# Moving a 288-byte table behind the big tiles: the same program with most on-chip addresses 96 bytes lower

## The chip, the cores and the metric

The kernel runs on one core of a Trainium2 chip. The metric is the device time of one execution in microseconds; the median of several runs is compared. A core has a matmul engine (TensorE, PE in the profile, with its weight loads as PEld), VectorE (DVE), ScalarE (ACT), GpSimd (POOL) and SyncE (SP). Each has a queue of its own, in which instructions start in order, and they wait for each other by semaphores. On-chip memory has 128 partitions; a tile occupies the same range of bytes in each of them. Transfers are issued from SP's, ACT's and POOL's queues and run on the 16 DMA engines of the core.

## The reference

Attention with a window of 128 keys and four sink keys, and then a mixture of four experts, in which every token uses all four, weighted by its gates.

```python
# q, k, v: (4, 8, 768, 64); domain_probs: (3072, 4); w1: (4, 512, 1024); w2: (4, 1024, 512)
scores = q @ k.T / sqrt(64)                       # per batch and head
keep = (key < 4) | ((0 <= query - key) & (query - key < 128))
a = softmax(where(keep, scores, -1e9))
x = (a @ v) as (3072, 512)                        # heads side by side
p = domain_probs / (domain_probs.sum(-1, keepdims=True) + 1e-9)
for e in range(4):
    out += p[:, e:e+1] * (relu(x @ w1[e]) @ w2[e])
```

## The kernel before

**Order of the work.** The kernel text is a planner. While it is built it keeps an estimated clock for each engine (the dictionary t), and at each step emits the piece of work that is ready and has the best priority: a step of attention, a first product (x by w1), or a second product (the hidden rows by w2). So the order on each engine is fixed when the program is built, from constants alone. Nothing in it looks at an address.

**Stages.** The four batches are worked through in turn, each in three groups of 256 tokens. Rows of q and k are loaded by GpSimd into the tiles qkn (L267, 128 bytes of bf16 per head and token) and, from the second batch on, turned into qkT by DMA transposes that SP issues (L276). Rows of v go to the six tiles vx (L331), in which a head takes 66 elements, 132 bytes. Scores come from L719, their exponent from L747 into aT, the masks from L739, the products with v from L789 into od; ACT scales them into onat (L834), and a DMA transpose makes xT (L806). For most units (256 tokens by one expert) both products are computed in a form with seven partial products instead of eight: L1336 and L1224 are first products of this kind, L1511 the second ones into acc. The sums that it needs are formed by VectorE: L1384 and L1399 in the first product, L1451 and L1428 on the hidden rows in H.

**Turned units.** A unit of later batches is either computed with hidden features in partitions, and then its gates are a row tile (gates0, filled by L491), or turned: with tokens in partitions. Then the gate of a token is one number per partition, read from the table own_gates at L1357 (ACT) or L1361 (DVE), and the finished half unit is brought into H by a DMA transpose at L1317. Its source is one of a few half-unit tiles: row, rest, or lent space of gates. own_gates is loaded once, when attention reaches the second batch, at L1634, and normalised by four short VectorE instructions.

**Spaced row loads.** For the later batches GpSimd places a copy of two elements into the tile held before each row load (L212 and L1726). The copy reads something that another engine has just made, and so holds the load back until then.

**Tiles.** Pools are laid out in the order in which they are opened: consts, wpool, attn_sb, moe_sb, odd. Within a pool tiles follow each other in the order of their creation, each rounded up to 32 bytes. The pool consts holds vx0 to vx5 (1,056 bytes each), own_gates (288), the row gates, ident, masks and the sink keys. Then come the weights, the attention tiles and the mixture's tiles, nearly all of 256 bytes times a whole number, and behind them, in odd, what is small or uneven.

The lines at the centre, cut where dots stand, with their numbers:

```python
325     vx = [consts.tile([P, H, DP], BF16, name=f"vx{tb}") for tb in range(NQB)]
327     own_gates = consts.tile([P, OWNED, E], FP32, name="own_gates")
...
276     nc.sync.dma_start(out=qkT[b][:, :, :, tb * P:(tb + 1) * P]..., in_=nat[b, tb]..., transpose=True)
331     nc.gpsimd.dma_start(out=vx[tb][:, :, 0:D], in_=v[b, :, tb * P:(tb + 1) * P, :].rearrange("h p d -> p h d"))
...
1317    nc.sync.dma_start(out=H[:, k]..., in_=X[k]..., transpose=True)
1361    nc.vector.tensor_scalar(out=X[k][:, :, s], in0=src, scalar1=0.0, scalar2=gate, op0=ALU.max, op1=ALU.mult)
1384    nc.vector.tensor_add(tiles["V"], c5, tiles["X"])
1451    x[0](*x[1:])          # one of three sums: S0 = H21 + H22, S1 = S0 - H11, H21 = H11 - H21
```

The unit's tiles["V"] of L1384 is what the products P7 and P3 of the same unit are added to, so PE waits for it. L1451 runs when all of H has landed.

Of the kernel before, what the change touches and what calls it, by code (L numbers as in the profile page):

```python
# [11 lines left out]
FP32 = mybir.dt.float32  # L12
BF16 = mybir.dt.bfloat16
# [3 lines left out]
def kernel(  # L17
# [17 lines left out]
    E, Dm, F = moe_w1.shape  # L35
    Ntok, Dout = out.shape

    P = 128
# [7 lines left out]
    NHP = H // 2  # L46
# [52 lines left out]
    NEARLY = 2  # L99
# [39 lines left out]
    def dve(cols, *deps, rate=0.96, fixed=157):  # L139
        at = max([t["dve"], *deps])  # L140
        t["dve"] = at + fixed - 77 + cols / rate
        return at + fixed + 60 + cols / rate

    def pool(cols, *deps, fixed=190):
        at = max([t["pool"], *deps])
        t["pool"] = at + fixed + cols * 1.8
        return t["pool"] + 35
# [96 lines left out]
    consts = ctx.enter_context(tc.tile_pool(name="consts", bufs=1))  # L244
# [3 lines left out]
    odd = ctx.enter_context(tc.tile_pool(name="odd", bufs=1))  # L248
# [75 lines left out]

    vx = [consts.tile([P, H, DP], BF16, name=f"vx{tb}") for tb in range(NQB)]
    OWNED = 2 * NG * (B - OWN)
    own_gates = consts.tile([P, OWNED, E], FP32, name="own_gates")

    def load_v(b, ts):
        for tb in ts:  # L330
            nc.gpsimd.dma_start(  # L331
                out=vx[tb][:, :, 0:D],
                in_=v[b, :, tb * P:(tb + 1) * P, :].rearrange("h p d -> p h d"),
            )
            lands(("v", b, tb), H * P, D, values_at[b - 1, min(NG - 1, (tb + 1) // 2)] if b else 0.0)
# [159 lines left out]
        gate_at[pair, e] = sp(mix.finished[mix.gated[len(gate_sb) - 1 - NGATE]] if len(gate_sb) > NGATE else 0.0, takes=300) + GATE_LANDS  # L495


    held = odd.tile([P, 2], BF16, name="held")
    nc.vector.memset(identf, 1.0)
    lent = wpool.tile([P, 12 * P], BF16, name="lent", tag=f"wf_{E - 2}")  # L500
    zeros = lent[:, 0:4 * P]
# [4 lines left out]
    for h in range(H):  # L506
# [1 line left out]
        nc.sync.dma_start(  # L508
            out=vsf[r:r + NSINK, :, 0:D], in_=v[:, h, 0:NSINK, :].rearrange("b j d -> j b d"),
        )  # L510
    scale_t = odd.tile([P, 2 * NEARLY, E], FP32, name="scale_t")
    ident = consts.tile([P, P], BF16, name="ident")
    load_v(0, (0,))
    for sgn in (1, -1):
# [2 lines left out]
            base=0, pattern=[[sgn, P]], channel_multiplier=-sgn,  # L517
        )
        pool(0, fixed=320)
    sel2 = odd.tile([P, NHP, 2], FP32, name="sel2")  # L520
    load_v(0, (1,))
    t["sw"] += 500
    for tb in (2, 3):
# [52 lines left out]
    t["dve"] += 240.0  # L576

    vsd = {}
    half = odd.tile([P, 2], BF16, name="half")
    ksd = [consts.tile([P, NHP, 32], BF16, name=f"ksd{i}") for i in range(2)]  # L580

    nc.vector.memset(half, 0.0)
# [375 lines left out]


    def gates():  # L960
        rs = odd.tile([P, 2 * NEARLY], FP32, name="rs")
        nc.vector.reduce_sum(out=rs, in_=scale_t, axis=AX.X)
        nc.vector.tensor_scalar_add(out=rs, in0=rs, scalar1=1e-9)
        nc.vector.reciprocal(out=rs, in_=rs)
        nc.vector.tensor_mul(scale_t, scale_t, rs[:, :, None].to_broadcast([P, 2 * NEARLY, E]))
        dve(200)
# [8 lines left out]
    class Mixture:  # L975
# [608 lines left out]
        def emit_second(self):  # L1584
            ready = self.second_ready()
            g, s, e = self.second.pop(0)
            if g not in out_sb:
                out_sb[g] = mo.tile([P, 2, Dout], FP32, name="osbw", tag=f"wide{g}", bufs=1)
                if g == 0:
                    gates()  # L1590
# [232 lines left out]
```

## Time and profile before

| what | value |
|---|---|
| median of the runs | 353.84 us (353.64 to 354.11) |
| the profiled execution | 356.82 us, of which the span is 355.1 |
| granted TensorE clock | 1.00 |
| instructions | 8,924 |
| moved by DMA | 47.95 MB in 173,606 packets, 158,084 of them under 512 bytes |
| DMA queue of GpSimd (q0) | 79,104 packets, 56.9% of 16 engines' span |
| DMA queue of SP (q1) | 93,404 packets, 47.3% of 16 engines' span |

The page of a profile gives the busy time of each engine, the span in 40 slices with the busy share in tenths, the DMA queues, the chain of work that ended last, and the costliest groups of instructions, each by its line, engine, operation and tiles. The two shares of the DMA queues can add up to more than the busy time of the engines, since the packets of one queue take longer when the other's are served between them. The span runs from the first to the last instruction; the time of an execution is a little longer.

### The profile page before, as it was taken

To read this page: it belongs to the slowest core of one execution; us is meant where nothing else is said; L and a number is where in the kernel's file an instruction comes from. 1 tells how busy PE (TensorE), PEld (TensorE's weight loads), DVE (VectorE), ACT (ScalarE), POOL (GpSimd) and SP (SyncE) were. 2 spreads that over 40 slices of the span, in tenths; PEclk is the share of its full clock that TensorE was granted. 3 is DMA by queue.
4 is the path that set the end of the run, shared out by engine and by line. 5 is a ranking of instruction groups with operands and counts; after the bars stand their busy time and mean duration, and the time that the engine had idled before them with its cause. 6 is when DMAs were issued, how large, how long until landed. Compare 5 with 4: busy or idle time off the path is not lost. (4 is left out here: it accounts for less than half of the span.)

```text
span 355.1 us, 8924 instructions
## 1 busy us (share of the span) xinstructions
PE 344.3 (97%) x3439; PEld 256.0 (72%) x3470; DVE 276.0 (78%) x661; ACT 215.5 (61%) x491; POOL 80.6 (23%) x125
## 2 busy tenths in 40 slices
PE   7999999999999999999999979999999999999996
PEld 3685769756788978786997736855856666666785
DVE  5792999988998999798699479669859595685740
ACT  4865714447656576658545569489678666757511
POOL 8946114330452540800252110000000000000000
PEclk9999999999999999999999999999999999999999
DMA  9999999999997999994899957538527938455431
GB/s 173 173 189 194 220 207 172 170 152 162 172 110 77 170 181 170 145 121 41 95 190 111 167 105 144 95 83 141 104 73 145 162 70 160 79 97 141 85 95 61
DMA packets 173606, 47.95 MB, mean 135 GB/s; under 512 B 158084, under 2 KB 169572, under 8 KB 173564
## 3 DMA queue, kind: packets, MB, share of 16 engines
q0 software_dynamic: 79104, 17.31, 56.9%
q1 hardware_dynamic: 93404, 29.55, 47.3%
q10 hardware_dynamic: 1056, 0.52, 0.5%
q8 instruction: 27, 0.44, 0.5%
q14 instruction: 15, 0.12, 0.1%
HBM read 37.61 MB, written 6.34 MB: 124 GB/s over the span
## 5 line engine op out<-in xcount | busy, mean ns | idle before, releaser
L1511 PEld LDWEIGHTS <-H 128*128 128x128 bf16 x708 | 66.4, 98 | 21.3 <-issue 2.5
L1511 PE MATMUL acc<-w,H 128*128 128x256 bf16 x420 | 57.4, 273 | 0.7 <-ACT acc L1550 0.5
L747 ACT ACTIVATE aT<-sps 128x512 bf16<-128x512 f32 (+1 forms) x96 | 47.0, 574 | 7.0 <-PE sps L719 5.5
L1354 ACT ACTIVATE cps<-cps 128x512 f32<-128x512 f32 x51 | 29.7, 588 | 23.0 <-PE cps L1336 22.1
L1511 PEld LDWEIGHTS <-S 128*128 128x128 bf16 x320 | 30.6, 98 | 9.4 <-issue 0.6
L1336 PE MATMUL cps<-w,T 128*128 128x512 bf16 x99 | 29.9, 379 | 3.1 <-DVE cps L1384 3.0
L1134 PE MATMUL hps<-xT,w 128*128 128x256 bf16 x256 | 32.1, 273 | 0.1
L834 ACT ACTIVATE onat<-od,R 128x64 bf16<-128x64 f32 x108 | 24.9, 326 | 9.5 <-DVE R L816 9.3
L1511 PE MATMUL acc<-wf,H 128*128 128x256 bf16 (+1 forms) x216 | 29.7, 271 | 0.1
L1336 PEld LDWEIGHTS <-T 128*128 128x128 bf16 x208 | 19.6, 98 | 14.0 <-issue 3.8
L1224 PEld LDWEIGHTS <-w 128*128 128x128 bf16 x448 | 28.2, 98 | 2.1
L1597 PE MATMUL acc<-w,H 128*128 128x512 bf16 x121 | 29.2, 379 | 0.4
L1336 PE MATMUL cps<-vf,T 128*128 128x512 bf16 x98 | 29.3, 379 | 0.2
L1336 PE MATMUL cps<-w,xT 128*128 128x512 bf16 x94 | 28.1, 379 | 0.2
L1377 ACT COPY cps<-cps 128x512 f32<-128x512 f32 x26 | 15.0, 578 | 20.6 <-PE acc L1511 11.7
L1134 PEld LDWEIGHTS <-w 128*128 128x128 bf16 x256 | 24.2, 98 | 4.3 <-issue 0.4
L1572 ACT COPY osb<-acc 128x256 f32<-128x256 f32 x35 | 13.4, 382 | 21.8 <-PE acc L1511 21.8
L331 POOL DMA_DIRECT2D vx<-in_v_dram x24 | 21.5, 899 | 17.1 <-PE tx L853 4.7
L739 DVE TENSOR_TENSOR aT<-aT,masks 128x1024 bf16<-128x1024 bf16 (+1 forms) x36 | 22.8, 644 | 3.1 <-ACT aT L747 2.8
L1257 DVE SCALAR_TENSOR_TENSOR H<-cps,gates 128x512 bf16<-128x512 f32 x36 | 24.2, 684 | 0.0
L267 POOL DMA_DIRECT2D qkn<-in_q_dram x22 | 19.4, 882 | 12.7 <-DMA w<-in_moe_w_dram 6.0
L1224 PEld LDWEIGHTS <-vf 128*128 128x128 bf16 x336 | 20.5, 98 | 1.4 <-issue 0.3
(154 smaller groups left out, 697.1 us busy)
## 6 DMA issues: line engine op xcount, KB each, us to landing
w<-in_moe_w_dram POOLq DMA_DIRECT2D x6, 1024.0 KB, 18.2
out_dram<-osb SPq DMA_DIRECT2D x17, 256.0 KB
vx<-in_v_dram POOLq DMA_DIRECT2D x24, 128.0 KB, 6.4
qkn<-in_q_dram POOLq DMA_DIRECT2D x22, 128.0 KB, 7.4
qkn<-in_k_dram POOLq DMA_DIRECT2D x22, 128.0 KB, 7.3
gates<-gate_rows SPq DMA_DIRECT2D x14, 128.0 KB
w<-in_moe_w_dram POOLq DMA_DIRECT2D x4, 256.0 KB, 7.4
w<-in_moe_w_dram POOLq DMA_DIRECT2D x2, 512.0 KB, 11.6
```

The source lines that it names most:

```text
L267: nc.gpsimd.dma_start(out=nat[b, tb][:, i], in_=(q, k)[i][b, :, tb * P:(tb + 1) * P, :].rearrange("h p d -> p h d"),)
L331: nc.gpsimd.dma_start(out=vx[tb][:, :, 0:D], in_=v[b, :, tb * P:(tb + 1) * P, :].rearrange("h p d -> p h d"),)
L739: nc.vector.tensor_mul(x, x, m[:, None, :].to_broadcast([P, 2 if g == 0 else 4, w if g == 0 else 2 * P]))
L747: nc.scalar.activation(out=a[:, ph], in_=sps[ph][:, 0:w], func=AF.Exp, scale=scale)
L834: nc.scalar.mul(o[:, qi, hp, ph * D:(ph + 1) * D], od[:, qi, ph, 0:D], R[:, qi, ph])
L1134: nc.tensor.matmul(h[:, i].rearrange("p (q n) -> p q n", q=2), lhsT=w1_sb[e][:, db, fb * P:(fb + 1) * P], rhs=xT[b, g][:, :, db], start=(i ...
L1224: nc.tensor.matmul(y[:, f], lhsT=A[:, d, f * P:(f + 1) * P], rhs=T[:, d], start=(m in ("P1", "P5") and f == 0 and d == 0), stop=(d == 1), ...
L1257: nc.vector.scalar_tensor_tensor(out=dst, in0=src, scalar=0.0, in1=gate, op0=ALU.max, op1=ALU.mult)
L1336: nc.tensor.matmul(y.rearrange("p f n -> p (f n)"), lhsT=T[:, d], rhs=A[:, d], start=(m in ("P1", "P5") and d == 0), stop=(d == 1), skip_g ...
L1354: nc.scalar.activation(out=src, in_=src, func=AF.Relu)
L1511: nc.tensor.matmul(y, lhsT=self.operand(b, g, e, m)[:, f], rhs=forms[e][m][:, f, cs], start=(k == 0 and f == 0 and m in (("P1", "P5", "P2" ...
L1597: nc.tensor.matmul(op, lhsT=H[:, fb // QF, fb % QF, s], rhs=w2_sb[e][:, fb, :], start=(fb == 0), stop=(fb == NFB - 1),)
```

## The change

The table own_gates is created in the last pool, odd, and no longer in consts. Five small tiles that lay in odd are created in consts, right behind vx: scale_t (64 bytes per partition), sel2 (32), held, half and rs (32 each, after rounding up). All other text stays.

```diff
-    own_gates = consts.tile([P, OWNED, E], FP32, name="own_gates")
+    own_gates = odd.tile([P, OWNED, E], FP32, name="own_gates")
+    scale_t = consts.tile([P, 2 * NEARLY, E], FP32, name="scale_t")
+    sel2 = consts.tile([P, NHP, 2], FP32, name="sel2")
+    held = consts.tile([P, 2], BF16, name="held")
+    half = consts.tile([P, 2], BF16, name="half")
+    rs = consts.tile([P, 2 * NEARLY], FP32, name="rs")
...
-    held = odd.tile([P, 2], BF16, name="held")
...
-    scale_t = odd.tile([P, 2 * NEARLY, E], FP32, name="scale_t")
...
-    sel2 = odd.tile([P, NHP, 2], FP32, name="sel2")
...
-    half = odd.tile([P, 2], BF16, name="half")
...
     def gates():
-        rs = odd.tile([P, 2 * NEARLY], FP32, name="rs")
```

As the program is built, the addresses in a partition are these:

| tiles | before | after |
|---|---|---|
| vx0 to vx5 | 16,512 to 22,847 | the same |
| own_gates | 22,848 | 226,560 |
| scale_t, sel2, held, half, rs | between 226,656 and 229,231 | 22,848 to 23,039 |
| gates0 | 23,136 | 23,040 |
| every tile from gates0 to osb1 | 96 past a multiple of 256 | a multiple of 256 |

## The prediction

> **What bounds the kernel now.** I read the page's engine rows first, then the waits of TensorE (PE), and then, for the one large wait, the timeline back from it.
>
> ```profile
> PE 344.3 (97%) x3439; PEld 256.0 (72%) x3470; DVE 276.0 (78%) x661; ACT 215.5 (61%) x491; POOL 80.6 (23%) x125
> PE   7999999999999999999999979999999999999996
> DMA  9999999999997999994899957538527938455431
> ```
>
> PE is busy for 97% of the span, in all slices but the first, one at about 204 us, and the last. The DMA engines are full for the first half and no longer after that. So the bound is the PE stream, and a layout of the on-chip memory can win only what PE loses in waits, unless it changes what one matmul costs. These are PE's waits of the whole span, from the view of waits:
>
> ```profile
> PE cps L1336 <- DVE cps L1384: 3.0, 2, 2.5
> PE acc L595 <- DVE lent L502: 1.4, 1, 1.4
> PE acc L1511 <- ACT acc L1550: 0.5, 1, 0.5
> PE tr L616 <- DVE qkn L300: 0.3, 1, 0.3
> PE tx L853 <- DVE onat L819: 0.2, 1, 0.2
> ```
>
> The five add up to 5.4 us. The 1.4 is the start, before any of the moved tiles matters (a VectorE memset must come first). The 3.0 is two waits for VectorE (DVE), 2.5 and 0.5. The timeline around the larger one shows what DVE itself waited for:
>
> ```profile
> 186.36 10.87 SPq L276 DMA_TRANSPOSE qkT<-qkn  x3
> 197.32 1.47 SPq L806 DMA_TRANSPOSE xT<-onat  x1
> 198.88 2.65 SPq L1317 DMA_TRANSPOSE H<-row  x2
> ...
> 200.52 0.88 POOL L331 DMA_DIRECT2D vx<-in_v_dram  x1 [0.34 <-issue]
> ...
> 204.51 0.42 DVE L1451 TENSOR_TENSOR S<-H 128x512 bf16<-128x512 bf16 x1 [4.65 <-DMA H<-row]
> ...
> 205.98 0.69 DVE L1384 TENSOR_TENSOR cps<-rest,cps 128x512 f32<-128x512 f32 x1
> ...
> 206.72 0.59 PE L1336 MATMUL cps<-w,T 128*128 128x512 bf16 x2 [2.50 <-DVE cps L1384]
> ```
>
> Read from the bottom: PE sat 2.50 us for the addition at L1384. That stood in DVE's queue behind the sums at L1451, and the first of them sat 4.65 us until a DMA transpose of a turned unit had landed in H. Six transposes stood on SP's queue from 186.36 to 201.53, and a row load for vx (200.52) ran into the last of them. The smaller wait has the same root:
>
> ```profile
> ACT row L1390 <- DMA H<-row: 1.1, 1, 1.1
> DVE cps L1384 <- ACT row L1390: 0.9, 1, 0.9
> PE cps L1336 <- DVE cps L1384: 0.5, 1, 0.5
> ```
>
> Here ScalarE (ACT) waits for a transpose, DVE for ACT, PE for DVE. So 3.0 us of PE's time hang on when transposes land, and nothing else that a tile's place could touch is late for PE.
>
> **What the change does.** It removes no instruction and adds none: each engine keeps its stream, and each wait its place. Only addresses change. Ahead of the big pools the table own_gates (288 bytes per partition) goes, and scale_t, sel2, held, half and rs come in (64, 32, 32, 32 and 32 bytes, small ones rounded up to 32), so every tile from gates0 to osb1 moves down by 288 - 192 = 96 bytes, from 96 past a multiple of 256 to a multiple of 256. The six vx tiles stay where they are, and the few small tiles behind osb1 shift by 32 to 160 bytes. The number of bytes moved, the DRAM side, PSUM and the sizes of all operands stay.
>
> **Instructions of the engines: 0.** The trace has one group of matmuls whose moving rows come from tiles that lie at six different places (vx, 1,056 bytes apart, with heads 132 bytes apart), and DVE's sums in H, which all lie at 96:
>
> ```profile
> L789 PE MATMUL od<-vx,aT x352: 190/193/204, 8.9 to 274.3; 128*128 128x65 bf16 x176
> L1451 DVE TENSOR_TENSOR S<-H x35: 396/421/437, 94.5 to 335.9; 128x512 bf16<-128x512 bf16 x35
> ```
>
> 352 matmuls over all these places lie within 190 to 204 ns, with a median of 193. Were the place of a row worth anything to PE, the group would split. I take 0, for DVE and ACT as well, though the trace has no DVE group of one shape at two places. The bounds: the spread of the matmuls, 14 ns, cannot be excluded on either side, but their median lies 3 ns above the fastest. A loss or gain of 1 ns on each of 3,439 matmuls would be 3.4 us; I give it no case of its own; the range, which reaches 2.5 us down and 1.7 up, holds most of it. The small tiles that move (held, the table as a per-partition scalar) are read a few bytes at a time by the same instructions: 0. The table's one load waits for nobody new.
>
> **Row loads: 0, at most an advantage that PE doesn't feel.** The loads of q and k rows (128 bytes per head, into qkn) get aligned; those of v have the same size, and their rows start at all sorts of places both before and after:
>
> ```profile
> vx<-in_v_dram POOLq DMA_DIRECT2D x24, 128.0 KB, 6.4
> qkn<-in_q_dram POOLq DMA_DIRECT2D x22, 128.0 KB, 7.4
> qkn<-in_k_dram POOLq DMA_DIRECT2D x22, 128.0 KB, 7.3
> ```
>
> The crooked tile is no slower to land (6.4 us) than the regular one (7.4). That speaks for no price on the side of the writes. The most that could go is the gap between them, 1.0 us for one load; PE waits for no load, so it would only let transposes be issued sooner.
>
> **Transposes: a little, and this is the term of the sum.** One transpose moves 1,024 rows of 256 bytes, 256 KB; each row starts at 96 before and at 0 after, so it covers parts of two blocks of 256 bytes before and one after. A lone transpose was issued at 262.80, a lone store of as many bytes in rows of 2 KB at 205.76:
>
> ```profile
> 262.80 1.23 SPq L1317 DMA_TRANSPOSE H<-row  x1
> ...
> 205.76 0.33 SPq L1558 DMA_DIRECT2D out_dram<-osb  x1
> ...
> 264.00:265.40 1.40, 1.40 (x18) 0.94 (x16) 0.55 (x1) 1.40 (x4) 0.00 (x0) 1.00 0.97 186
> 206.30:207.70 1.40, 0.98 (x5) 0.48 (x5) 0.72 (x2) 0.00 (x0) 0.95 (x2) 1.00 0.49 187
> ...
> L1317 SPq DMA_TRANSPOSE H<-row x19: 1231/1237/2292, 134.6 to 324.6; - x19
> ```
>
> The next-to-last number of a window is the mean share of the 16 DMA engines: 0.97 of 1.40 us, so 1.36 us for the transpose; 0.49 of 1.40, so 0.69 us for the store. The difference, 0.67 us, is the price of having eight times as many rows, and whatever the straddling costs is inside it: 0 to 0.67 us for one transpose. The nearest row for a choice is that of the loads, which show no price at all, so I go near the lower end. A second bound comes from the issue: SP takes at least 1,231 ns for each, so in a run of back-to-back transposes each can gain no more than 1.36 - 1.23 = 0.13 us. I take 0.1 us. For the run of six that ends in the 2.50 us wait that is 6 x 0.1 = 0.6 us earlier for the sum at L1451, and PE's wait shrinks by as much. The ends: 0; and, if the full 0.67 comes off the last one, 5 x 0.13 + 0.67 = 1.3 us, with more only if the row load stops being in the way (below). The wait of 0.5 us depends on one transpose: at most 0.1 of it, within the rounding.
>
> [...]
>
> **Sum.** The profiled execution took 356.82 us (span 355.1 and 1.7 around it): 356.82 - 0.6 = 356.2. It lies 2.98 us above the median of 353.84, close to the 3.0 us of the two waits, so the undisturbed runs may have less of these waits, or the profiling itself costs the rest; the trace cannot say. Taken over to the median: 353.84 - 0.6 = 353.2 us, 0.17% less. A difference under 0.2%, 0.7 us, is about what a measurement of this kernel can't tell from none.
>
> **Rivals.**
> - *The alignment counts in full.* [...]
>
> ```profile
> 201.00:203.00 2.00, 1.95 (x13) 1.11 (x13) 0.00 (x0) 1.07 (x2) 0.40 (x1) 1.00 0.94 174
> 203.00:204.50 1.50, 1.23 (x6) 0.47 (x5) 0.00 (x0) 1.04 (x3) 0.00 (x0) 1.00 1.36 86
> ```
>
>   From 203.0 on the moved bytes halve (174 to 86 GB/s) while the engines are full: that is the load's small rows, and DVE was released only at 204.5, when they were through. With 1.3 us from above and this 1.5, the 2.50 goes altogether, and the 0.5 with it: 353.84 - 3.0 = 350.8. Against it: the loads' 6.4 and 7.4, and that the undisturbed runs may not have these waits. Chance 0.20.
> - *A row load meets another transpose (slower).* Transposes release loads as well as sums:
>
> ```profile
> POOL held L1726 <- DMA qkT<-qkn: 27.0, 2, 15.6
> ```
>
>   Two trains of row loads start when the last qkT transpose of a batch lands; if that comes sooner, the loads move against SP's other transposes, for which DVE and then PE wait. The price is that of the meeting seen above, 1.5 us on the landing, where DVE has no other work ready: 353.84 + 1.5 = 355.3, and as much as 2.5 (356.3) if it falls as badly as at 204 us. It decides where a shift of a few tenths puts a load in front of a transpose that is on the chain; PE has no slack to hide it. Against it: the shift is small, and most transposes have a wait of DVE or ACT in hand. Chance 0.24.
> - *Nothing at all.* The place of a row has no price, and each engine does what it did: 353.84. Chance 0.10.
>
> **Chances and range.** My forecast, a gain of 0 to 1.3 us around 0.6, has 0.46, of which 0.18 lies beyond 0.7 us. Faster by over 0.2%: 0.18 + 0.20 = 0.38. Within 0.2%: 0.28 + 0.10 = 0.38. Slower: 0.24. The forecast's own range is 352.5 to 353.8. The range for 8 in 10 leaves out half of the first rival and the worse third of the second: 351.3 to 355.5.
>
> **What would show it.** In the profile after, a lone transpose's DMA time (share times window) at 1.2 to 1.3 us instead of 1.36, SP's issue still 1.23, matmuls of 512 columns still at their mean, and PE's wait for L1384 below 2.5. A transpose at 1.0 us or less, with no PE wait near 204 us, would prove the first rival; a new wait of PE whose chain ends at a transpose beside a row load the second. I am wrong altogether if a group of PE, DVE or ACT instructions has another mean than before, or if the time moves by over 1 us with transposes of the same length.

## The result, and the profile after

The changed kernel takes 352.79 us (median of 19 runs, 352.11 to 354.39), the kernel before 354.43 us beside it (19 runs, 353.40 to 356.30). The ratio is 0.9957, with a 95% interval of 0.9945 to 0.9970: some 0.4% faster, 1.6 us between the medians where 0.6 was forecast. When both were run again with other kernels (change_again, below) the ratio was 0.998, so the medians put the size at 0.2 to 0.4%, and the two intervals together reach from 0.06 to 0.55%. Three single runs far above the others of their kernel (358.79, 358.88 and 1,260 us) are left out of every comparison below.

The profiled execution of the kernel before (356.82 us) was slower than every one of these 19 runs; that of the kernel after (352.58) lies a little below its median. So 4.2 us between the two profiles stand for 1.6 between the kernels, and what differs between them is partly chance.

Engine rows, slices and DMA queues of the page after:

```profile
PE 345.4 (98%) x3470; PEld 256.2 (73%) x3470; DVE 275.8 (79%) x661; ACT 215.3 (61%) x491; POOL 79.8 (23%) x125
PE   8999999999999999999999999999999999999996
...
q0 software_dynamic: 79104, 17.31, 56.7%
q1 hardware_dynamic: 93404, 29.55, 44.8%
```

The slice at 204 us is full now. The weight loads (PEld) number 3,470 in both traces, so the 3,439 matmuls of before lack 31 records and are no smaller stream. SP's queue q1, which carries the transposes, took 44.8% of the span of the DMA engines where it took 47.3%, with the same packets and bytes; POOL's queue q0, which carries the row loads, 56.7 instead of 56.9. In another execution of the changed kernel (change_again) the two are 43.5 and 54.5, so between two single profiles a point or two can be chance. Of the PE waits these are left (view of waits, whole span: us in total, times, longest):

```profile
PE acc L596 <- DVE lent L506: 1.4, 1, 1.4
PE cps L1336 <- DVE cps L1384: 0.3, 1, 0.3
PE tx L854 <- DVE onat L820: 0.2, 1, 0.2
```

5.4 us became 1.9, so 3.5 of the 4.2 us between the two profiles stand in these waits. The 3.0 at L1384 are 0.3, and ACT's 0.5 at L1550 is gone. The timeline, at the place of the 2.50 us wait, after:

```profile
194.65 2.81 SPq L1317 DMA_TRANSPOSE H<-row  x2
...
199.08 0.88 POOL L336 DMA_DIRECT2D vx<-in_v_dram  x1 [0.34 <-issue]
...
199.31 0.43 DVE L1451 TENSOR_TENSOR S<-H 128x512 bf16<-128x512 bf16 x1 [0.89 <-DMA H<-row]
...
201.60 0.70 DVE L1384 TENSOR_TENSOR cps<-rest,cps 128x512 f32<-128x512 f32 x1 [0.74 <-PE cps L1336]
```

The two transposes start 4.23 us earlier than in the trace of before (198.88), POOL's load follows them as it did, and DVE waits 0.89 us for H, not 4.65. At L1384 it is now DVE that waits for PE.

Six transposes that are 0.2 us shorter each cannot give 4.23 us, and they did not. The first of the six is issued 2.18 us earlier (184.18, before 186.36). Most of the rest lies in what the merged line of three qkT transposes hides: its 10.87 us before (9.03 after) are three issues of 1.23 us and, between them, waits for the row loads of k. SP's waits between the three issues, before (188 to 198 us) and after (186 to 194), and the third issue, before:

```profile
SPq L276 <- DMA qkn<-in_k_dram: 7.1, 2, 4.0
```

```profile
SPq L276 <- DMA qkn<-in_k_dram: 5.2, 2, 4.5
```

```profile
196.00 1.23 SPq L276 DMA_TRANSPOSE qkT<-qkn  x1
```

So the six were no run of transposes back to back: the transposes into H stood in SP's queue behind one that stood for a row load.

A transpose that has the DMA engines to itself, after: SP's issue by the timeline, and the window over its packets (the next-to-last number is the mean share of the 16 DMA engines):

```profile
258.61 1.23 SPq L1317 DMA_TRANSPOSE H<-row  x1
...
259.70:261.00 1.30, 1.30 (x18) 0.94 (x16) 0.34 (x1) 1.30 (x4) 0.00 (x0) 1.00 0.90 202
```

0.90 x 1.30 = 1.17 us of DMA time, where it was 1.36. The issue is 1.23 as before. The matmuls did not change (groups by line: least, median and most ns; two groups after, then L1336 before):

```profile
L790 PE MATMUL od<-vx,aT x352: 190/193/204, 8.7 to 270.1; 128*128 128x65 bf16 x176
...
L1336 PE MATMUL cps<-w,T x104: 376/379/390, 127.1 to 329.9; 128*128 128x512 bf16 x104
```

```profile
L1336 PE MATMUL cps<-w,T x99: 376/379/390, 128.3 to 334.1; 128*128 128x512 bf16 x99
```

DVE's sums on H have a median of 415 ns, where the trace of before has 421. After, and then in table_moved_at_96 (below), where H lies at 96 as before:

```profile
L1451 DVE TENSOR_TENSOR S<-H x35: 391/415/426, 94.0 to 331.7; 128x512 bf16<-128x512 bf16 x35
```

```profile
L1452 DVE TENSOR_TENSOR S<-H x35: 395/418/426, 95.3 to 335.5; 128x512 bf16<-128x512 bf16 x35
```

So two executions with H at 96 differ by 3 ns (421 and 418) already; whether the place has a share in the 6 ns between 421 and 415 is not shown.

### The profile page after: what moved, and what is told of

Read it like the earlier page. It is cut to its first block, busy times and chain, and to the rows that moved or that the text cites. A ratio compares the mean times of both kernels' runs of the same rounds, so it can differ in the third digit from the quotient of the medians.

```text
span 350.9 us, 8955 instructions
## 1 busy us (share of the span) xinstructions
PE 345.4 (98%) x3470; PEld 256.2 (73%) x3470; DVE 275.8 (79%) x661; ACT 215.3 (61%) x491; POOL 79.8 (23%) x125
## 3 DMA queue, kind: packets, MB, share of 16 engines
q0 software_dynamic: 79104, 17.31, 56.7%
q1 hardware_dynamic: 93404, 29.55, 44.8%
## 4 chain that ended last, share of the span: by engine, by line
PE 94%; DVE 3%; DMA 1%; ACT 1%; issue 1%; DVEq 0%; ACTq 0%
PE acc L1511 34%; PE cps L1336 22%; PE cps L1224 12%; PE acc L1597 8%; PE hps L1134 7%; PE sps L720 3%; PE od L790 3%; PE acc L596 2%; DMA H<-row 1%; PE od L783 1%; DVE aT L758 1%; PE tx L854 1%; DVE onat L820 0%; PE tr L617 0%; PE sinks L681 0%
## 5 line engine op out<-in xcount | busy, mean ns | idle before, releaser
L1511 PEld LDWEIGHTS <-H 128*128 128x128 bf16 x708 | 66.4, 98 | 20.7 <-issue 1.9
L1511 PE MATMUL acc<-w,H 128*128 128x256 bf16 x420 | 57.4, 273 | 0.0
L1511 PEld LDWEIGHTS <-S 128*128 128x128 bf16 x320 | 30.6, 98 | 9.4 <-issue 0.6
L1336 PE MATMUL cps<-w,T 128*128 128x512 bf16 x104 | 30.9, 379 | 0.3 <-DVE cps L1384 0.3
L1336 PE MATMUL cps<-vf,T 128*128 128x512 bf16 x104 | 30.6, 379 | 0.0
L1336 PE MATMUL cps<-w,xT 128*128 128x512 bf16 x104 | 30.3, 379 | 0.0
L1511 PE MATMUL acc<-wf,H 128*128 128x256 bf16 (+1 forms) x216 | 29.7, 271 | 0.0
L1336 PEld LDWEIGHTS <-T 128*128 128x128 bf16 x208 | 19.6, 98 | 11.1 <-issue 0.8
L267 POOL DMA_DIRECT2D qkn<-in_k_dram x22 | 20.0, 911 | 7.7 <-DMA w<-in_moe_w_dram 6.6
```

Of the source, the lines that this page charges most:

```text
L267: nc.gpsimd.dma_start(out=nat[b, tb][:, i], in_=(q, k)[i][b, :, tb * P:(tb + 1) * P, :].rearrange("h p d -> p h d"),)
L1336: nc.tensor.matmul(y.rearrange("p f n -> p (f n)"), lhsT=T[:, d], rhs=A[:, d], start=(m in ("P1", "P5") and d == 0), stop=(d == 1), skip_g ...
L1511: nc.tensor.matmul(y, lhsT=self.operand(b, g, e, m)[:, f], rhs=forms[e][m][:, f, cs], start=(k == 0 and f == 0 and m in (("P1", "P5", "P2" ...
```

## The experiments

All kernels but transposes_alone have the instructions and waits of the changed kernel; only addresses differ, so line numbers shift by one or two. Diffs are against the changed kernel. "At 96" means 96 bytes past a multiple of 256.

**Is it the table, or the place of the big tiles?** Two kernels part these. In table_stays the table remains in front of the big pools, which still begin at multiples of 256 because rs is moved back; in table_moved_at_96 the table moves, and a pad puts the big pools back to 96.

```diff
# table_stays
-    own_gates = odd.tile([P, OWNED, E], FP32, name="own_gates")
+    own_gates = consts.tile([P, OWNED, E], FP32, name="own_gates")
-    rs = consts.tile([P, 2 * NEARLY], FP32, name="rs")
+    rs = odd.tile([P, 2 * NEARLY], FP32, name="rs")
# table_moved_at_96
+    pad = consts.tile([P, 24], FP32, name="pad")
```

> The table own_gates stays in the front pool, and four of the five small tiles join it there (rs stays behind), so that every big tile starts at a multiple of 256 again. Theory 1, it is the place of the big tiles against blocks of 256 bytes: ratio to the kernel before as in the change, 0.994 to 0.998, and a lone transpose of a half unit at 1.17 us of DMA time (share times window), as in the profile after, against 1.36 before. Theory 2, it is the place of the table or of the small tiles: ratio 1.00, and 1.36 us.

> The change as it is, with 96 empty bytes behind the small tiles, so that the table lies behind the big pools and every big tile starts at 96 past a multiple of 256 as in the kernel before. Theory 1 (blocks of 256 bytes): ratio 1.000, within 0.002, a lone transpose at 1.36 us. Theory 2 (the table's place): ratio 0.994 to 0.998.

Measured: table_stays 353.00 us, ratio to the kernel before 0.9971 (0.9959 to 0.9984); table_moved_at_96 354.29 us, 1.001 (0.9993 to 1.0027). The table's place has no effect that shows; the place of the big tiles carries the gain.

**Which places are bad?** Pads, or three small tiles left in odd, put all big tiles at 64 or at 128. A transposed row of 256 bytes crosses a multiple of 256 at both; a loaded row of 128 bytes does so at 64 (every second row), but never at 128. This is meant of the rows of q and k; those of v go to vx, which stays in place in every kernel here.

```diff
# big_tiles_at_64
+    pad = consts.tile([P, 16], FP32, name="pad")
# big_tiles_at_128
-    scale_t = consts.tile([P, 2 * NEARLY, E], FP32, name="scale_t")
-    sel2 = consts.tile([P, NHP, 2], FP32, name="sel2")
-    held = consts.tile([P, 2], BF16, name="held")
+    scale_t = odd.tile([P, 2 * NEARLY, E], FP32, name="scale_t")
+    sel2 = odd.tile([P, NHP, 2], FP32, name="sel2")
+    held = odd.tile([P, 2], BF16, name="held")
```

> As the change, but scale_t, sel2 and held go back behind the big pools, so that every big tile starts at 128 past a multiple of 256. Rows of 256 bytes still lie over two blocks of 256, but at a multiple of 128 and 64. Theory 1 (blocks of 256): as the kernel before, ratio 1.000, a lone transpose at 1.36 us. Theory 3 (a finer grid, 64 or 128 bytes, is what counts): as the change, 0.996, and 1.17 us.

> As the change with 64 empty bytes behind the small tiles, so that every big tile starts at 64 past a multiple of 256. Theory 1 (blocks of 256): ratio 1.000 and 1.36 us for a lone transpose. Theory 3 with a grid of 64 bytes: 0.996 and 1.17 us; with a grid of 128 bytes: 1.000 and 1.36 us.

Measured: at 64 354.43 us, 1.0009 (0.9994 to 1.0025), nothing left of the gain; at 128 353.55 us, 0.9977 (0.9964 to 0.9991), about half of what table_stays gained beside it. Yet at 128 a lone H<-row is as long as before the change. Windows over such a transpose, in big_tiles_at_128:

```profile
260.60:262.20 1.60, 1.60 (x19) 1.09 (x18) 0.58 (x1) 1.60 (x4) 0.00 (x0) 1.00 0.86 164
```

0.86 x 1.60 = 1.38 us. So the transposes are not shorter here, and half of the gain is there all the same. That does not fit the forecast, whose only term they were, and pointed to the row loads. The comparison at 64 and 96 against 128 is the clearest on them: in runs taken side by side, with every transpose reading across in all three kernels, the two in which loaded rows cross lie 0.95 ± 0.46 us above the one in which they do not (difference of means, with twice its standard error).

**What does a place cost one transfer by itself?** In transposes_alone the kernel's work is left out (its output is zeros). It chains 100 transposes of 256 KB, each starting when the last has landed, with source and destination at 0, 32, 64, 96 and 128 in all 25 combinations; then row loads of 128 KB one at a time at these places; then two loads beside two transposes.

```diff
+    def turn(d, s):
+        nc.sync.dma_start(out=dst[d], in_=src[s], transpose=True)
...
+    pairs = [(d, s) for d in PLACES for s in PLACES]
+    for j, (d, s) in enumerate(pairs):
+        for i in range(4):
+            turn(d, s)
+            nc.vector.tensor_copy(out=src[s][:, 0:2], in_=last(dst[d]))
...
+    for n in PLACES:
...
+        for i in range(4):
+            load(row[n], i)
+            nc.vector.tensor_copy(out=row[n][:, 0, 0:2], in_=last(row[n]))
...
```

> Not the kernel but its transfers alone; its output holds zeros. One DMA transpose at a time (1,024 rows of 256 bytes) from tiles at 0, 32, 64, 96 and 128 past a multiple of 256 to tiles at the same five places, each waiting for the one before; then one row load at a time (rows of 128 bytes) to the five places; then two row loads beside two transposes, at 0 and 0, 0 and 96, 96 and 0, 96 and 96, 128 and 128, 64 and 64. Theory 1a (it is the writes that straddle a block of 256): a transpose to a tile at 0 lands about 0.3 us sooner than one to 32, 64, 96 or 128, whatever the source's place. Theory 1b (the reads): the same with source and destination changed over. Theory 1c (either): only 0 to 0 is sooner. A row load by itself: equal within 0.1 us at all places, if rows that straddle cost nothing without other traffic; beside transposes, 0 and 0 the fastest, by 0.5 us or more against 96 and 96, and 128 and 128 between them.

The groups by line; s is a source, d a destination, r a row tile; zero is 0, six 64, nine 96 and twelve 128. The last numbers of a line are VectorE's idle time for four transfers, ended by their landing:

```profile
L72 DVE COPY szero<-dnine 128x2 bf16<-128x2 bf16 x4 | 0.7, 172 | 11.4 <-DMA dnine<-szero 11.4
...
L72 DVE COPY ssix<-dsix 128x2 bf16<-128x2 bf16 x4 | 0.7, 172 | 12.6 <-DMA dsix<-ssix 12.6
...
L72 DVE COPY snine<-dzero 128x2 bf16<-128x2 bf16 x4 | 0.7, 172 | 12.7 <-DMA dzero<-snine 12.7
L72 DVE COPY stwelve<-dzero 128x2 bf16<-128x2 bf16 x4 | 0.7, 172 | 12.6 <-DMA dzero<-stwelve 12.6
...
L82 DVE COPY rzero<-rzero 128x2 bf16<-128x2 bf16 x4 | 0.7, 172 | 15.2 <-DMA rzero<-in_q_dram 7.8 <-DMA rzero<-in_k_dram 3.7 <-DMA rzero<-in_v_dram 3.7
L82 DVE COPY rnine<-rnine 128x2 bf16<-128x2 bf16 x4 | 0.7, 172 | 15.7 <-DMA rnine<-in_q_dram 8.0 <-DMA rnine<-in_v_dram 3.9 <-DMA rnine<-in_k_dram 3.8
...
L82 DVE COPY rtwelve<-rtwelve 128x2 bf16<-128x2 bf16 x4 | 0.7, 171 | 14.8 <-DMA rtwelve<-in_q_dram 7.5 <-DMA rtwelve<-in_k_dram 3.7 <-DMA rtwelve<-in_v_dram 3.6
```

For a transpose whose source is at 0 VectorE waits 11.3 to 11.4 / 4 = 2.85 us, wherever its destination lies; from 32, 64, 96 or 128 it waits 12.6 to 13.0 / 4 = 3.15 to 3.25. (The pair 0 to 0 runs first, beside VectorE's memsets, and only its last three waits count: 2.85 each.) Here it is the side that is read that counts: one step of 0.3 us, not graded between 32 and 128. A lone row load costs 3.7 to 3.9 us at every place, with no order by crossing beyond 0.2. In the rounds of two loads beside two transposes VectorE waited for the loads 52.7 us in eight rounds that load to 0, 51.5 in eight to 96, 27.0 in four to 64 and 26.7 in four to 128: 6.6, 6.4, 6.75 and 6.7 us a round, with no order by crossing. So here the price of a crossing row load, if it has one, does not show.

**The same inside the kernel: the read and the written side apart.** In hidden_rows_at_96 H (and osb, which no transpose touches) moves to 96, so that the transposes of turned units write there; in half_units_at_96 the tiles row0 and row1, from which 20 of the 52 transposes of turned units read, move to 96.

```diff
# hidden_rows_at_96 (ahead of H)
+            mo.tile([P, 24], FP32, name="pad", tag="pad", bufs=1)
# half_units_at_96
+    odd.tile([P, 16], FP32, name="pad")
+    rows = [odd.tile([P, F // 256, 2, P], BF16, name=f"row{i}") for i in range(HALVES)]
-            self.resting = [(0.0, mo.tile([P, QF, 2, P], BF16, name=f"row{i}", tag=f"row{i}", bufs=1)) for i in range(HALVES)]
+            self.resting = [(0.0, x) for x in rows]
```

> The change with 96 empty bytes ahead of the six tiles H: H, osb0 and osb1 start at 96 past a multiple of 256, all other big tiles at 0. So transposes into H write at 96 and read at 0; those into qkT and xT have both at 0. Theory 1a (writes): a lone transpose H<-row takes 1.36 us of DMA time, as before the change; the time lies between, ratio to before 0.997 to 1.000. Theory 1b (reads): 1.17 us and ratio 0.996.

> The change with the two tiles row, the source of 20 of the 52 transposes of turned units, moved behind the big pools to 96 past a multiple of 256; all other big tiles stay at 0. Theory 1a (writes): a lone H<-row takes 1.17 us of DMA time, and the ratio to before is 0.996 as in the change. Theory 1b (reads): a lone H<-row takes 1.36 us, while a lone H<-rest in the same run takes 1.17; ratio 0.996 to 0.998.

Measured: 353.02 us, 0.9966 (0.9950 to 0.9983), and 352.88 us, 0.9962 (0.9944 to 0.9979). Both keep the whole gain. Windows over lone transposes, in half_units_at_96 first one from a row tile at 96, then one from a tile named rest at 0:

```profile
260.60:262.10 1.50, 1.50 (x19) 1.03 (x17) 0.55 (x1) 1.50 (x4) 0.00 (x0) 1.00 0.91 175
269.00:270.40 1.40, 1.40 (x13) 1.06 (x12) 1.40 (x4) 1.40 (x6) 0.00 (x0) 1.00 0.83 187
```

0.91 x 1.50 = 1.37 us and 0.83 x 1.40 = 1.16 us, in one execution. In hidden_rows_at_96, which writes at 96, the same window gives:

```profile
261.40:262.70 1.30, 1.30 (x18) 0.96 (x17) 0.31 (x1) 1.30 (x4) 0.00 (x0) 1.00 0.89 202
```

0.89 x 1.30 = 1.16 us. So the step is on the read side in the kernel too; and 20 longer transposes cost no time that can be measured. SP's queue shows the step in sum: q1 has 47.0 to 47.6% of the span in the four profiles of kernels in which every transpose reads across (before, table_moved_at_96, big_tiles_at_64 and _at_128), and 43.5 to 44.9% in the four in which none does (the change twice, table_stays, hidden_rows_at_96).

**The row loads apart from the rest.** In three kernels the six qkn tiles, which the loads of q and k write, lie at 96, at 128 or at 64, and all other big tiles at 0; in a fourth qkn lies at 0, and everything from qkT to osb1 at 96. The changed kernel was run once more beside three of them.

```diff
# loaded_rows_at_96; the pad is 24 for _at_128 and 8 for _at_64
-            nat[b, tb] = sb.tile([P, 2, H, D], BF16, name="qkn", tag="qkn", bufs=NQB)
+            nat[b, tb] = odd.tile([P, 2, H, D], BF16, name="qkn", tag="qkn", bufs=NQB)
...
+    odd.tile([P, 16], FP32, name="pad")
...
# all_but_loaded_rows_at_96 (behind qkn)
+    sb.tile([P, 24], FP32, name="pad", tag="pad", bufs=1)
```

> The change once more, beside the three that follow. All theories: ratio to before 0.994 to 0.998.

> The change with the six tiles qkn, into which the rows of q and k are loaded and from which the qkT transposes read, moved behind the big pools to 96 past a multiple of 256; all other big tiles stay at 0. Theory 4 (the row loads that straddle, 128 bytes each, make up the part of the gain that the tiles at 128 kept): ratio 0.999 to 1.001, and SP's and POOL's queues as before the change, q0 at 57% or more of the span. Theory 5 (the qkT transposes, read from qkn, are the ones that count): 0.998 to 1.000 too, so this run alone does not tell 4 from 5. If neither counts: 0.996.

> As the run before, with qkn at 128 past a multiple of 256: no row of 128 bytes lies over two blocks of 256, while the qkT transposes still read rows that do. Theory 4: ratio 0.996 to 0.997 and q0 at 55 to 56.5%, clearly below the run with qkn at 96. Theory 5: as with qkn at 96, 0.998 to 1.000.

> The change with 96 empty bytes behind the six tiles qkn: the weights, masks and qkn stay at 0, everything from qkT to osb1 goes to 96. The 18 transposes into qkT read aligned rows, the 61 others, from onat, row, rest and gates, read straddling ones except where their source lies in qkn or the gates' tiles. Theory 4 or 5: ratio 0.996 to 0.997, since row loads and qkT transposes are as in the change. If it is the transposes of turned units and of xT that count: 0.999 to 1.001.

> The changed kernel with only the six qkn tiles at 64 past a multiple of 256; weights, masks, qkT, H and the half units stay at multiples. At 64, as at 96 and unlike 128, every second row of 128 bytes that a load writes crosses a multiple of 256. Theory (the gain hangs on loaded rows that cross): nearly all of it is lost, ratio 0.999 to 1.001 to the kernel before, some 0.5 us above the changed kernel, and ACT waits 1 us or more for POOL's held copies at 96 us with PE then losing some 0.5 us to ACT's addition at L1550. Rival (96 was a place bad by chance, or the difference was noise; the gain hangs on the transposes of H and xT): ratio 0.9955 to 0.998.

| kernel | us | ratio to before | loaded rows cross | transposes read across |
|---|---|---|---|---|
| change_again | 353.21 | 0.998 (0.9965 to 0.9994) | no | no |
| all_but_loaded_rows_at_96 | 353.11 | 0.998 (0.9968 to 0.9993) | no | those of xT and H |
| loaded_rows_at_128 | 353.09 | 0.9975 (0.9953 to 0.9997) | no | those of qkT, some of H |
| loaded_rows_at_96 | 353.71 | 0.9997 (0.9985 to 1.0009) | yes | those of qkT, some of H |
| loaded_rows_at_64 | 353.52 | 0.9990 (0.9977 to 1.0004) | yes | those of qkT, some of H |

With crossing loads about half of the gain goes, at 96 and less clearly at 64; with the same tiles at 128 it stays. The DMA queue of GpSimd, which was to tell them apart, does not: q0 has 56.5% at 96, 55.1 at 128 and 54.7 at 64. One interval alone does not part these kernels from each other, so I put the runs of all experiments together by what crosses. The differences are of means, with twice their standard error:

| what crosses | kernels | runs | mean us | above the first row |
|---|---|---|---|---|
| nothing | the change, change_again, table_stays | 43 | 353.00 | |
| row loads (with their qkT transposes) | loaded_rows_at_96, _at_64 | 24 | 353.66 | 0.66 ± 0.31 |
| transposes, no row load | all_but_loaded_rows_at_96, big_tiles_at_128, loaded_rows_at_128, half_units_at_96 | 47 | 353.20 | 0.20 ± 0.28 |
| both | the kernel before, table_moved_at_96, big_tiles_at_64 | 151 | 354.19 | 1.20 ± 0.21 |

hidden_rows_at_96, where only written rows cross, has 352.98. The part of the row loads is clear of zero, and so is the comparison of the runs side by side above. That of the transposes is not: big_tiles_at_128 lies 0.57 ± 0.43 above table_stays, which ran beside it, but all_but_loaded_rows_at_96 and loaded_rows_at_128 lie at change_again, which ran beside them, and half_units_at_96 lies at hidden_rows_at_96 (means). The two parts add up to 0.86 of 1.20; the rest is within the errors. The rows mix runs on different chips, and the mean of the kernel before alone goes from 353.96 to 354.38 between one experiment and another, so the sizes are rough.

**Where the slower executions lose it.** The profile of loaded_rows_at_96 is of an execution of 354.98 us, and it has a wait that the changed kernel's has not. Waits between 95 and 103 us, before, then loaded_rows_at_96:

```profile
ACT aT L747 <- POOL held L212: 1.4, 2, 1.0
...
PE acc L1511 <- ACT acc L1550: 0.5, 1, 0.5
```

```profile
ACT aT L749 <- POOL held L212: 1.4, 2, 1.0
...
PE acc L1512 <- ACT acc L1551: 0.5, 1, 0.5
```

The same stretch in loaded_rows_at_128 and in the kernel after:

```profile
POOL held L212 <- DVE S L1452: 0.4, 1, 0.4
```

```profile
POOL held L212 <- DVE S L1451: 0.4, 1, 0.4
```

Where the wait exists, ACT stands for POOL's spacing copies of the row loads, its addition at L1550 is late, and PE loses 0.5 us to that. These copies stand in POOL's queue behind one that waits for the last qkT transpose of the second batch, and SP issues that transpose when the rows for it have been loaded. Both by the timeline, before, after, and in loaded_rows_at_96:

```profile
85.72 2.53 SPq L276 DMA_TRANSPOSE qkT<-qkn  x1
...
92.88 0.52 POOL L1726 COPY held<-qkT 128x2 bf16<-128x2 bf16 x1 [15.62 <-DMA qkT<-qkn]
```

```profile
84.68 2.29 SPq L276 DMA_TRANSPOSE qkT<-qkn  x1
...
91.91 0.19 POOL L1726 COPY held<-qkT 128x2 bf16<-128x2 bf16 x1 [15.67 <-DMA qkT<-qkn]
```

```profile
85.57 2.01 SPq L276 DMA_TRANSPOSE qkT<-qkn  x1
...
92.93 0.59 POOL L1727 COPY held<-qkT 128x2 bf16<-128x2 bf16 x1 [16.20 <-DVE H L1258]
```

In these profiles the transpose is issued 0.9 to 1.0 us later where the rows cross, and the copy starts 1.0 us later. (In the last the profile names DVE as what came last, an instruction that ended just then.) But this is not a wait that crossing rows cause every time. The profile of loaded_rows_at_64, of an execution of 352.53 us, has transpose and copy early, and no such wait:

```profile
84.58 2.46 SPq L276 DMA_TRANSPOSE qkT<-qkn  x1
...
91.70 0.19 POOL L1727 COPY held<-qkT 128x2 bf16<-128x2 bf16 x1 [15.19 <-DMA qkT<-qkn]
```

The wait is in all five profiles of executions above 354 us (before, table_moved_at_96, big_tiles_at_64, hidden_rows_at_96, loaded_rows_at_96), and in none of the eight of executions below. In the five the copy starts at 92.45 us or later, in the eight at 92.00 or earlier; and one of the five, hidden_rows_at_96, has no loaded row that crosses. Above 354 us were 68 of 128 runs of the kernel before, 8 of 24 with crossing loads alone, 4 of 43 with nothing crossing. These are no two kinds of execution, though: the runs of each group lie around one centre with the same spread (a standard deviation of 0.6 us), and the centre moves. None of the 128 runs of the kernel before is below 353.02 us, 23 of the 43 with nothing crossing are. The wait of 0.5 us is a sign of a late execution, not the whole of what it loses. Where the rest goes shows in the last qkT transpose, for which SP waits until its rows are loaded: SP issues it at 196.0 us in the profile before and at 192.0 in the one after, and from there to the end of the execution it is 160.8 and 160.6 us. Ten profiles (all but before, table_moved_at_96 and loaded_rows_at_64) have a chain that ended last in which the same 44 products of L1511 take 4.91 us at about this place: they start at 194.6 to 196.0 us in the seven of executions below 354 us and at 196.6 to 197.2 in the three above, and from there to the end of the execution it is 157.7 to 157.8 us in all ten. So what an execution loses it has lost by then, in the part of the kernel in which the row loads run. That is seen in the profiles, not tried: no run took a wait away by itself.

## Why the prediction was right, and where it was not

**What bounds the kernel: right.** PE stayed the bound, at 98% of the span, and 3.5 of the 4.2 us between the two profiles stand in PE's waits.

**Instructions, 0: right.** The 128x65 matmuls take 193 ns in both traces, the 512-column ones 379, though every weight tile moved. By its letter the last sign, that another mean of a DVE group would make the forecast wrong altogether, did come: 415 ns for 421. But two executions with H at 96 have 421 and 418, and the sign left no room for what differs between executions.

**Transposes, 1.36 to 1.2 or 1.3 us: right in the length, unsure in what it brings.** The lone one measures 1.17, a little under the forecast; SP's issue stayed at 1.23. As a term of the sum they had 0.6 us; the runs give 0.20 ± 0.28, and the comparisons of runs side by side 0.57 once and otherwise nothing. The carrier was not what the text said, either. Six times 0.1 us presumes six transposes back to back, and SP waited for row loads between them, 7.1 us in the trace of before. And the 2.50 us wait at their end belongs to the one execution that was profiled: table_moved_at_96, with the big tiles at the same places past a multiple of 256, waits 0.5 us at L1384 in its whole span:

```profile
PE hps L1135 <- ACT sinkA L690: 0.8, 1, 0.8
PE cps L1337 <- DVE cps L1385: 0.5, 1, 0.5
PE acc L1512 <- ACT acc L1551: 0.5, 1, 0.5
```

The prediction had noted that the profiled run lay 2.98 us above the median, about the size of those waits, and still let its term rest on them. That was the weak point of the argument.

**Row loads, 0: the step that failed.** "At most an advantage that PE doesn't feel" measured 0.66 ± 0.31 us, the larger term. It is 0.95 ± 0.46 in the comparison of runs side by side. The forecast argued from landing times, vx's 6.4 us against qkn's 7.4. They don't tell: qkn's loads take 7.3 on the page after and 6.3 in change_again, the same kernel, and in loaded_rows_at_64, where they cross, the page has

```profile
qkn<-in_q_dram POOLq DMA_DIRECT2D x22, 128.0 KB, 6.6
qkn<-in_k_dram POOLq DMA_DIRECT2D x22, 128.0 KB, 6.4
```

A median landing time can hide the few loads that something hangs on. And "PE waits for no load" overlooked the waits with another name. The 0.5 us at L1511 stood in the quoted list and was not followed back: PE for ACT, ACT for POOL's held copy, POOL for a transpose, the transpose for a load. The 2.50 us was followed back to a transpose and no further; the next step, in SP's queue, is a row load again.

**The size: partly luck.** The time of 352.79 us lies in the forecast's own range, but the gain of 1.6 us beside the kernel before lies above its upper end of 1.3, and that of 0.9 in the second comparison within it. The term that carried the forecast brought the smaller part, and the one put at 0 the larger.

**The rivals.** Alignment in full (350.8) did not come: not 3.0 us but 0.9 to 1.6 went, and the 204 us wait was no property of the kernel. The second, row loads that meet transposes, had the right two parties but the wrong sign: loads and transposes did both come sooner in the profile after, and no new wait for a transpose took the place. (The profile of loaded_rows_at_128 has one, of 1.0 us for a qkT transpose, in an execution of 353.77 us.) Nothing at all is excluded by the interval.

**The landing.** In the chain of transposes alone those that read from 0 landed 0.3 us sooner than the others (2.85 us against 3.15 to 3.25), more than the 0.19 us by which the DMA time of a lone one fell in the kernel (1.36 to 1.17). Where the rest of the 0.3 comes from was not shown.

**What stays open.** Why the crossing row loads cost time in the full kernel, when alone and beside two transposes they cost none that shows. That the writes matter, and not the transposes which read the same tiles, rests on the kernels at 128 against those at 96 and 64: clear when all big tiles move, with overlapping intervals when qkn alone does. How the loads' delay reaches PE is followed in single profiles and tried in none. Nor did the runs settle whether the transposes' share is nearer to 0 or to 0.6.

## What to carry to other kernels

Lay out tiles that DMA transposes read, or that many short rows are loaded into, so that no row crosses a multiple of 256 bytes, and measure it; here, with rows of 256 and 128 bytes, it cost a reordering of small tiles and was worth 0.2 to 0.4%, of which only the loads' part is clear of zero. Before a forecast rests on a single large wait, see how far the profiled run lies from the median: a wait as large as that distance may be no part of the kernel. Follow also the small waits back through two or three engines, and through the queue that issues the DMAs, since a load can be late for TensorE without its name in TensorE's row, as behind the 0.5 us at L1511 here. A merged line of the timeline (x3) can hold waits between its instructions: 7.1 of 10.87 us here.

## What the runs showed of the hardware

One after the other, DMA transposes of 256 KB made VectorE wait 2.85 us each for the landing when their source rows start at a multiple of 256 bytes and 3.15 to 3.25 us at 32, 64, 96 or 128 past it; the destination made no difference, and neither did how far past it is. In the kernel one takes 1.16 to 1.17 us of DMA time from 0 and 1.36 to 1.38 from 96 or 128. Row loads of 128-byte rows landed in 3.7 to 3.9 us at every place by themselves, and the full kernel was 0.66 ± 0.31 us slower in the mean all the same where they crossed, for a reason that stays open. Addresses alone moved the runs of one and the same program by some 1.2 us: none of 128 below 353.02 us with the big tiles at 96, 23 of 43 with them at 0.
